# The two half tiles at the end of a fused attention-and-MLP kernel write their results into another pair of SBUF buffers

## The chip, the cores and the metric

The kernel runs on one core of a Trainium2 chip. The metric is device time in microseconds for one execution, from start to end, the median of several runs. The engines of the core that matter here are TensorE (PE, matrix products into PSUM), VectorE (DVE, which reads PSUM and writes SBUF), and SyncE (SP), whose queue issues nearly all DMA transfers, the stores of the output among them.

## The reference, cut to what matters

The input `x` has 2048 tokens of 512 numbers in bf16. It is normalised per token, and two branches read the result: an attention with a running memory (32 heads of 16, four segments of 512 tokens, causal softmax inside a segment, a memory of the earlier segments mixed in by a gate), and an MLP with SiLU (512 to 1792 to 512). The output is the sum of both and `x`.

```python
def _A_ref(x, wq, wk, wv, wo, beta):
    ...
    for s in range(N):                                   # N = 4 segments of L = 512
        p = _softmax(einsum('bhqd,bhkd->bhqk', qs, ks) * scale + mask, axis=-1)
        a_dot = einsum('bhqk,bhkd->bhqd', p, vs)
        num = einsum('bhld,bhde->bhle', phi(qs), M)
        den = einsum('bhld,bhd->bhl', phi(qs), z)[..., None] + 1e-06
        outs.append(g * (num / den) + (1.0 - g) * a_dot)
        M = M + einsum('bhld,bhle->bhde', phi(ks), vs)
        z = z + einsum('bhld->bhd', phi(ks))
    ...
    return o @ wo

def _B_ref(x, w1, w2):
    return _silu(x @ w1) @ w2

x = A_x
xn = _layernorm(x, axis=-1)
return x + _A_ref(xn, A_wq, A_wk, A_wv, A_wo, A_beta) + _B_ref(xn, B_w1, B_w2)
```

## The kernel before, in words

The 2048 tokens are 16 token tiles of 128, four to each of the four segments (`s` = 0 to 3, `j` = 0 to 3 inside a segment). Every matrix product is computed with 128 rows on the partitions. The last step for a token tile adds 18 products in one PSUM bank: 14 of the MLP (`hT`, one for each 128 of the 1792 hidden numbers, with `w2_sb`) and 4 of the attention (`oT` with `wo_sb`). `out_mm` (line 624) issues one such product, whole or in parts; `product` (line 329) splits it into four matmuls of 32 columns of the weights where the neighbouring products do so too, and at the end of the kernel all are split so (line 334).

When the 18 products of a tile are in, one VectorE instruction reads the bank, halves it, adds the residual `x` and writes bf16 into an SBUF buffer (line 617 in `store`), and SyncE issues a DMA from this buffer to the output in HBM (line 622). The last tile of the last segment (`s` = 3, `j` = 3) is done in two halves of 256 output columns instead: the words `oh<i>.<h>` are its products (`half_out`, line 656) and `sh0` and `sh1` its two stores (`half_store`, line 659: VectorE at line 664, the DMA at line 668). Half 0, half 1 and tile 2 lie in banks of their own of one PSUM tile (`psS`, line 637 and 638), and `declare_no_dep` (line 652) says that products in one of these banks need not wait for VectorE's reading of another.

SBUF buffers come from pools. A name (or `tag`) in a pool stands for a fixed number of equal buffers that are handed out in turn: whoever asks for one when all have been used gets the one that was handed out longest ago, and its first writer has to wait until the last reader of the old contents is done. The waits are put in by the framework, as semaphore waits on the instruction. In the pool `work`:

- `o_out` has 3 buffers of 128 x 512 bf16. They are used for the output tiles (line 616), and in the kernel before also for the two halves (line 663). The last reader of the old contents is a store's DMA, so the wait is for its completion.
- `pos` has 2 buffers (the pool's default) of 128 x 512 bf16. They hold the positive part of keys or queries: GpSimd writes it (line 413 in `phi_pos`), and VectorE reads it soon after (line 429 in `phi_sum`).

The order of all work is written out by hand: the string `ORDER` (lines 16 to 90) is a list of words, each word names a piece and its numbers, and the loop at line 900 issues the pieces in this order; each engine then runs its own instructions in that order. No scheduler moves them. The end of the string, cut to the words of the end:

```
... o3.0.15 st3.0 o3.2.17 o3.2.15 oh7.1 st3.2 od3.1.11.3 oh8.0 oh16.1 o3.1.17 o3.1.2 oh3.0 oh17.1 oh12.0 st3.1
oh4.1 oh15.0 oh17.0 oh1.0 oh16.0 sh0 oh3.1 oh10.1 oh15.1 oh0.1 oh5.1 sh1
```

So the last five output buffers are handed out to the tiles 0, 2 and 1 of the last segment (`st3.0`, `st3.2`, `st3.1`), to half 0 (`sh0`) and to half 1 (`sh1`), in this order. With three buffers in turn, half 0 gets the buffer of tile 0, and half 1 that of tile 2.

Of the kernel before, what the change touches and what calls it, by code (L numbers as in the profile page):

```python
# [10 lines left out]
BF16 = mybir.dt.bfloat16  # L11
# [82 lines left out]
def kernel(  # L94
# [15 lines left out]
    P = 128  # L110
    S = 2048
    D = 512
# [5 lines left out]
    L = S // NSEG  # L118
# [12 lines left out]
    work = ctx.enter_context(tc.tile_pool(name="work", bufs=2))  # L131
# [527 lines left out]
    def half_store(h):  # L659

        st, j, cols = sts[LAST], TPS - 1, slice(h * D // 2, (h + 1) * D // 2)
        assert len(st.pop(("done", j, h))) == 4 * (FT + DT)
        o_half = work.tile([P, D], BF16, name="o_half", tag="o_out", bufs=3)[:, 0 : D // 2]
        out = nc.vector.scalar_tensor_tensor(
            out=o_half, in0=st["psO", j, h], scalar=0.5, in1=st["x", j][:, cols], op0=ALU.mult, op1=ALU.add
        )
        fin_out.append(((j, h), out))
        nc.sync.dma_start(out=out_flat[(NT - 1) * P : NT * P, cols], in_=o_half)
# [188 lines left out]
    def keep_busy(n):  # L857
# [21 lines left out]
        "o": out_mm, "oh": half_out,  # L879
        "oc": lambda s, j, i, c: out_mm(s, j, i, None, c, 2), "od": lambda s, j, i, c: out_mm(s, j, i, None, c, 4),  # L880
        "sh": half_store, "xl": load_res, "st": out_store,
        "xs": ln_stats, "xc": ln_sums, "xd": ln_var, "xg": ln_root, "xq": ln_sqrt, "xi": ln_inv, "tb": first_exp,
        "Nv": lambda t: ln_norm(t, nc.vector), "Na": lambda t: ln_norm(t, nc.gpsimd),
# [55 lines left out]
```

## Time and profile before

| | |
|---|---|
| time before, median of 3 runs | 221.58 us (221.27 to 221.88) |
| the profiled execution: its own time | 221.36 us |
| the profiled execution: span from the first to the last instruction | 219.7 us |
| granted TensorE clock, mean over the span | 0.999 |
| PE busy | 211.5 us, 96% of the span |
| DVE busy | 181.2 us, 82% of the span |
| output stores of full tiles (line 622) | 15 of 128 KB |
| output stores of the halves (line 668) | 2 of 64 KB |

The times are of one execution on the chip, seen by the hardware profiler. The span is shorter than the run's time by 1.7 us, which lie before its first and behind its last instruction. A row of the timeline has the start and the length of a group of instructions in microseconds, then the engine, the line in the kernel, the operation, what it writes and what it reads, the shapes, and how many instructions are in the group (x4). An engine's name with a q behind it (SPq, DVEq) is that engine's instruction queue: the issuing of a DMA, a wait on a semaphore. In square brackets stands how long the engine had been idle before, and whose work ended this. The chain of work that ended last is followed back from the last instruction that counts as busy; DMAs that run on behind that instruction are not in it.

### The profile page before, as it was taken

Reading aid. Unit: us, or ns where it says so; the run is one execution under the profiler, and the core shown is the slowest. Engines: PE = TensorE matmul, PEld = TensorE weight load, DVE = VectorE, ACT = ScalarE, POOL = GpSimd, SP = SyncE. Lnnn points to the kernel's source line nnn. Section 1 sums busy time; section 2 is a strip of 40 time slices with the busy share of each in tenths; the row PEclk is TensorE's granted clock in tenths of the full one; section 3 lists DMA queues with packets and bytes.
Section 4 is the critical chain, followed back from the end, with each engine's and each line's share of the span. In section 5 each row is a group of like instructions: output and inputs, shape, how many; then the busy total and the mean of one; then the engine's idle time right before and its main releaser. Section 6 shows DMA issues by size and latency. Waiting matters only on the chain.

```text
span 219.7 us, 9344 instructions
## 1 busy us (share of the span) xinstructions
PE 211.5 (96%) x4019; PEld 116.2 (53%) x4042; DVE 181.2 (82%) x370; ACT 184.3 (84%) x173; POOL 126.8 (58%) x203
## 2 busy tenths in 40 slices
PE   7999999999999999999999999999999999999993
PEld 7666655556544444445544445555454554465662
DVE  7899899998897878766988978777899898678463
ACT  3899989999999999999999999999999998850000
POOL 6039986679687845695845586676768472410000
PEclk9999999999999999999999999999999999999999
DMA  5994549241003033221122141250032222312212
GB/s 185 364 387 116 78 112 345 57 82 44 3 4 75 27 90 86 68 56 31 48 75 63 46 116 28 50 76 7 4 96 88 66 75 51 99 52 86 88 51 97
DMA packets 32745, 19.60 MB, mean 89 GB/s; under 512 B 14656, under 2 KB 32192, under 8 KB 32704
## 3 DMA queue, kind: packets, MB, share of 16 engines
q1 hardware_dynamic: 30080, 16.39, 27.8%
q10 hardware_dynamic: 2624, 2.62, 3.8%
q8 instruction: 31, 0.51, 1.0%
q14 instruction: 10, 0.08, 0.1%
HBM read 9.96 MB, written 2.10 MB: 55 GB/s over the span
## 4 chain that ended last, share of the span: by engine, by line
PE 80%; DVE 10%; POOL 4%; issue 2%; DMA 1%; ACT 1%; DVEq 0%
PE ps L332 20%; PE psO L334 16%; PE ps L334 15%; PE psS L720 9%; PE psO L332 9%; PE psV L787 8%; PE psS L334 3%; DVE stats L282 2%; POOL Pb L740 2%; DVE Vz L402 1%; POOL k L381 1%; DMA out_dram<-o_out 1%; DVE hT L493 1%; DVE pk L429 1%; POOL lows L740 1%
## 5 line engine op out<-in xcount | busy, mean ns | idle before, releaser
L726 ACT ACTIVATE Pb<-psS 128x2048 bf16<-128x2048 f32 x72 | 135.2, 1877 | 6.2 <-PE psS L720 4.1
L740 POOL TENSOR_SCALAR_AFFINE_SELECT Pb<-Pb 128x512 bf16<-128x512 bf16 (+2 forms) x88 | 61.6, 709 | 19.4 <-ACT Pb L726 16.6
L493 DVE SCALAR_TENSOR_TENSOR hT<-th,ps 128x512 bf16<-128x512 bf16 x56 | 37.9, 680 | 10.4 <-ACT th L488 10.0
L740 POOL TENSOR_SCALAR_AFFINE_SELECT lows<-Pb 64x512 bf16<-64x512 bf16 (+1 forms) x40 | 23.2, 580 | 37.4 <-ACT Pb L726 31.0
L334 PE MATMUL psO<-w_sb,hT 128*32 128x512 bf16 (+2 forms) x708 | 43.3, 321 | 0.0
L332 PE MATMUL ps<-xnT,w_sb 128*128 128x512 bf16 (+1 forms) x165 | 34.2, 329 | 0.4 <-DVE Vz L402 0.2
L488 ACT ACTIVATE th<-ps 128x512 bf16<-128x512 f32 x56 | 33.2, 594 | 1.7 <-PE ps L334 1.6
L334 PEld LDWEIGHTS <-hT 128*32 128x32 bf16 x876 | 21.6, 97 | 14.0 <-issue 2.6
L334 PE MATMUL ps<-xnT,w_sb 128*32 128x512 bf16 (+1 forms) x448 | 26.4, 348 | 0.0
L720 PE MATMUL psS<-qT,k 32*128 32x64 bf16 (+3 forms) x512 | 23.0, 233 | 0.5 <-ACT Pb L726 0.3
L332 PEld LDWEIGHTS <-w_sb 128*128 128x128 bf16 x168 | 15.8, 98 | 11.5 <-issue 1.0
L787 PE MATMUL psV<-Pb,Vz 128*32 128x448 bf16 (+7 forms) x512 | 21.6, 286 | 0.2 <-POOL Pb L740 0.2
L720 PEld LDWEIGHTS <-k 32*128 32x128 bf16 x512 | 9.4, 92 | 22.8 <-issue 22.2
L332 PE MATMUL psO<-w_sb,hT 128*128 128x512 bf16 (+2 forms) x82 | 20.9, 326 | 0.6 <-issue 0.5
L787 PEld LDWEIGHTS <-Vz 128*32 128x32 bf16 x768 | 16.2, 97 | 9.3 <-issue 0.8
L617 DVE SCALAR_TENSOR_TENSOR o_out<-psO,x_res 128x512 bf16<-128x512 f32 x14 | 9.7, 690 | 6.6 <-PE psO L334 4.9
L334 PEld LDWEIGHTS <-w_sb 128*32 128x32 bf16 x448 | 11.1, 96 | 7.4 <-issue 1.6
L720 PE MATMUL psS<-qT,kT 16*128 16x448 bf16 (+3 forms) x256 | 14.7, 269 | 0.0
L817 DVE CAST oraw<-psV 128x512 bf16<-128x512 f32 x15 | 10.2, 682 | 3.1 <-PE psV L787 3.0
L402 DVE CAST Vz<-ps 128x512 bf16<-128x512 f32 x15 | 10.2, 681 | 2.8 <-PE ps L334 1.6
L332 PEld LDWEIGHTS <-hT 128*128 128x128 bf16 x89 | 7.8, 98 | 8.7 <-issue 2.2
L332 PE MATMUL ps<-xnT,wq_sb 128*128 128x256 bf16 (+1 forms) x59 | 12.1, 322 | 0.2 <-issue 0.2
(113 smaller groups left out, 333.5 us busy)
## 6 DMA issues: line engine op xcount, KB each, us to landing
spr<-rz SPq DMA_DIRECT2D x56, 64.0 KB
x_res<-in_A_x_dram SPq DMA_DIRECT2D x16, 128.0 KB
out_dram<-o_out SPq DMA_DIRECT2D x15, 128.0 KB
w_sb<-in_B_w_dram SPq DMA_DIRECT2D x1, 1792.0 KB
w_sb<-in_B_w_dram ACTq DMA_DIRECT2D x1, 1792.0 KB
x_hi<-in_A_x_dram SPq DMA_DIRECT2D x2, 512.0 KB
wv_sb<-in_A_wv_dram SPq DMA_DIRECT2D x2, 256.0 KB
wk_sb<-in_A_wk_dram SPq DMA_DIRECT2D x1, 512.0 KB
```

Of the source, the lines that this page charges most:

```text
L282: nc.vector.bn_stats(out=stats[t][:], in_=xs(t, t + 1)[:, 0, :])
L332: return [nc.tensor.matmul(out, lhsT=lhsT, rhs=rhs, start=start, stop=stop, skip_group_check=True)]
L334: nc.tensor.matmul(out[c : c + 32], lhsT=lhsT[:, c : c + 32], rhs=rhs, start=start, stop=stop, tile_position=(0, c), skip_group_check=True,)
L402: copy(out=Vzs[s % 2][:, j, :, 0:3:2, :], in_=sts[s].pop(("v", j))[:, :].rearrange("p (h r d) -> p h r d", r=2, d=DH),)
L488: nc.scalar.activation(out=th[:], in_=sts[s]["h", ft][:, :], func=AF.Tanh, scale=0.5)
L493: nc.vector.scalar_tensor_tensor(out=st["hT"][:, ft, :], in0=st.pop(("th", ft))[:], scalar=1.0, in1=st.pop(("h", ft))[:, :], op0=ALU.add, ...
L617: out = nc.vector.scalar_tensor_tensor(out=o_out[:], in0=st.pop(("psO", j)), scalar=0.5, in1=st["x", j][:], op0=ALU.mult, op1=ALU.add)
L720: nc.tensor.matmul(psS[:, g, c : c + q2 - q1], lhsT=keys[rows], rhs=st["qT"][rows, dt, q1:q2], start=True, stop=True, tile_position=(32 * ...
L726: exp = nc.scalar.activation(out=blocks(Pb, b).rearrange("p y g c -> p g y c"), in_=psS[:, :, :].rearrange("p g (y c) -> p g y c", c=BLOCK ...
L740: over[id(Pb)].append(nc.gpsimd.affine_select(out=out, in_=in_, compare_op=ALU.is_ge, fill=0.0, base=base, pattern=[[0, out.shape[1]], [1, ...
L787: nc.tensor.matmul(psV[32 * g : 32 * g + 32, q0 : q0 + nq].rearrange("p (y c) -> p y c", y=weights.shape[2]), lhsT=Vzs[s % 2][:, kt, 4 * d ...
L817: copy(out=oraw[:], in_=sts[s].pop(("psV", 0))[:, :])
```

## The change

Only line 663 differs. The buffer of a half is no longer taken from the three of `o_out`, but from the two of `pos`. The size of the buffer, the 256 of its 512 columns that are used, the instructions that write and store it, and their order stay.

```diff
         st, j, cols = sts[LAST], TPS - 1, slice(h * D // 2, (h + 1) * D // 2)
         assert len(st.pop(("done", j, h))) == 4 * (FT + DT)
-        o_half = work.tile([P, D], BF16, name="o_half", tag="o_out", bufs=3)[:, 0 : D // 2]
+        o_half = work.tile([P, L], BF16, name="o_half", tag="pos")[:, 0 : D // 2]
         out = nc.vector.scalar_tensor_tensor(
             out=o_half, in0=st["psO", j, h], scalar=0.5, in1=st["x", j][:, cols], op0=ALU.mult, op1=ALU.add
         )
```

`L` and `D` are both 512. The order of instructions on every engine is the same in both kernels; the two VectorE instructions of line 664 wait for PE, for an earlier VectorE instruction and for one DMA each in the kernel before, and for PE alone in the changed one.

## The prediction

> **What bounds the kernel now.** I read the head of the page first, then the chain of waits at its end, the timeline of the last microseconds by engine, and the transfers in slices. The page's head gives engines and span:
>
> ```profile
> span 219.7 us, 9344 instructions
> PE 211.5 (96%) x4019; PEld 116.2 (53%) x4042; DVE 181.2 (82%) x370; ACT 184.3 (84%) x173; POOL 126.8 (58%) x203
> ```
>
> TensorE is busy for 96% of the span, so it bounds the kernel nearly everywhere. The change doesn't touch its stream, but it touches the stretch in which TensorE no longer bounds. The chain of work that ended last, from 213 us on, as start, length and what:
>
> ```profile
> 213.47 0.02 issue
> 213.50 0.70 DVE o_out L617
> 214.20 0.02 issue
> 214.21 2.01 DMA out_dram<-o_out
> 216.22 0.03 issue
> 216.25 0.05 DVEq L664
> 216.30 0.04 issue
> 216.35 0.27 DVE o_half L664
> 216.61 0.08 issue
> 216.69 0.41 DVE o_half L664
> ```
>
> The chain leaves TensorE at 213.47. It runs through the eviction of tile 0, then through the whole store of tile 0 (2.01 us from its issue to its landing), and only then into the two evictions of the halves. A store stands on the path to a VectorE instruction because that instruction writes into the buffer that the store reads. The waits of the last 7 us say the same (the total in us, how often, the longest), and the row of line 664 gives the durations of its two evictions (least, median, most, in ns):
>
> ```profile
> DVE o_half L664 <- DMA out_dram<-o_out: 0.9, 1, 0.9
> L664 DVE SCALAR_TENSOR_TENSOR o_half<-psS,x_res x2: 414/418/423, 216.3 to 216.7; 128x256 bf16<-128x256 f32 x2
> ```
>
> VectorE sits idle for 0.9 us ahead of half 0. Now TensorE's last rows, and VectorE's and SyncE's:
>
> ```profile
> 215.28 0.28 PE L334 MATMUL psS<-wo_sb,oT 128*32 128x256 bf16 x4
> 215.39 0.39 PE L334 MATMUL psS<-w_sb,hT 128*32 128x256 bf16 x8
> 215.61 0.28 PE L334 MATMUL psS<-wo_sb,oT 128*32 128x256 bf16 x4
> 215.72 0.39 PE L334 MATMUL psS<-w_sb,hT 128*32 128x256 bf16 x8
> ...
> 214.74 0.69 DVE L617 SCALAR_TENSOR_TENSOR o_out<-psO,x_res 128x512 bf16<-128x512 f32 x1
> ...
> 215.46 0.33 SPq L622 DMA_DIRECT2D out_dram<-o_out  x1
> 216.80 0.33 SPq L668 DMA_DIRECT2D out_dram<-o_half  x1
> 217.22 0.38 SPq L668 DMA_DIRECT2D out_dram<-o_half  x1
> ```
>
> Read beside the order of the words, the row at 215.28 is the last product of half 0, number 16. The 20 matmuls from 215.39 on are the five products of half 1 behind it. So half 0 is complete in PSUM at 215.28 + 0.28 = 215.56, and half 1 at 215.72 + 0.39 = 216.11. VectorE has nothing to do from 214.74 + 0.69 = 215.43 on, and yet the halves start at 216.35 and 216.69. It is the buffer that both wait for, not the data.
>
> **The change part by part.** It moves no instruction on any queue: VectorE, SyncE, TensorE, ScalarE and GpSimd issue the same work in the same order. It takes the DMA wait (and the wait on an earlier VectorE write) off the two instructions of line 664. What is left is the wait for TensorE.
>
> *The new buffers.* The two `pos` buffers were last written by GpSimd and last read by VectorE. The rows of that tile, with first and last start at the end of the list of numbers:
>
> ```profile
> L413 POOL TENSOR_SCALAR pos<-qT x12: 607/614/616, 38.8 to 166.1; 128x512 bf16<-128x512 bf16 x12
> L429 DVE SCALAR_TENSOR_TENSOR phiQT<-ex,pos x12: 677/684/983, 46.7 to 170.8; 128x512 bf16<-128x512 bf16 x12
> ```
>
> The last reader starts at 170.8 us and takes at most 0.98 us, so both buffers have been free for over 40 us, and there are two of them for two halves: neither half waits for a store again. Nobody asks for a `pos` buffer behind the halves, so no one else is held up. Taking these buffers costs nothing.
>
> *Half 0.* It starts when TensorE's product 16 is in. What lies between a product's end and the eviction that waits for it: in the chain above TensorE ends at 213.47 and VectorE starts at 213.50; by the timeline, the row of that product and one earlier case:
>
> ```profile
> 213.05 0.39 PE L334 MATMUL psO<-wo_sb,oT 128*32 128x512 bf16 x4
> ...
> 213.50 0.69 DVE L617 SCALAR_TENSOR_TENSOR o_out<-psO,x_res 128x512 bf16<-128x512 f32 x1 [1.74 <-PE psO L334]
> ...
> 204.28 0.60 PE L334 MATMUL psO<-w_sb,hT 128*32 128x512 bf16 x8
> 204.94 0.69 DVE L617 SCALAR_TENSOR_TENSOR o_out<-psO,x_res 128x512 bf16<-128x512 f32 x1 [2.02 <-PE psO L334]
> ```
>
> 213.50 - 213.44 = 0.06 and 204.94 - 204.88 = 0.06. So half 0 starts at 215.62, ends 0.42 later at 216.04, and its store is issued 0.03 later (before: 216.35 + 0.42 = 216.77, issue at 216.80), at 216.07. SyncE's queue is free by then: the store of tile 1 ahead of it ends issuing at 215.46 + 0.33 = 215.79. Issuing takes 0.33 and the queue needs another 0.09 to the next (217.22 - 216.80 - 0.33), so it is ready for half 1's store at 216.49.
>
> *Half 1.* It starts at 216.11 + 0.06 = 216.17 (VectorE is free at 216.04), ends 0.41 later at 216.58, and its store is issued at 216.61. Before, that issue was at 217.22. So the last store leaves 0.61 us earlier. The bounds: if the eviction starts at the modelled end of the product itself, 0.67; if it needs 0.12 instead of 0.06 and 0.42 instead of 0.41, 0.54. I take 0.61, because both rows of the hand-over give 0.06.
>
> *The reading beside the writing.* Half 0 is now read from PSUM while TensorE still writes half 1 into another bank; before, TensorE had long stopped. Tile 1 is evicted at 214.74 in the same way, beside 256-wide products at their usual pace (0.11 us for each, from the row at 215.28 to that at 215.39 as from 215.61 to 215.72). I cost this at nothing; if it slowed the 20 last matmuls by a tenth, it would be 0.05.
>
> *The stores.* From the issue of the last store to the end of the span it is 219.7 - 217.22 = 2.48 us: start-up, data, receipt, and the closing barrier. Does this stay 2.48 when the halves come sooner behind the full tiles? The last three columns of the slices are granted clock, share of the DMA engines and GB/s:
>
> ```profile
> 215.50:215.70 0.20, 0.20 (x16) 0.20 (x8) 0.00 (x0) 0.00 (x0) 0.00 (x0) 1.00 0.22 67
> ...
> 216.70:216.90 0.20, 0.00 (x0) 0.00 (x0) 0.20 (x2) 0.00 (x0) 0.00 (x0) 1.00 0.09 26
> ...
> 217.50:217.70 0.20, 0.00 (x0) 0.00 (x0) 0.00 (x0) 0.00 (x0) 0.00 (x0) 1.00 0.21 61
> ...
> 218.30:218.50 0.20, 0.00 (x0) 0.00 (x0) 0.00 (x0) 0.00 (x0) 0.00 (x0) 1.00 0.32 85
> ```
>
> In the first slice, between two full ones, tile 0's store ends its data and tile 2's begins. The data of tile 1's store are through at about 216.75. Half 0's begin at about 217.65, 0.85 us behind their issue, and half 1's are through by about 218.4; the 0.42 us between the two issues were enough to keep the two apart. With the change half 0's data begin at 216.07 + 0.85 = 216.92, still behind tile 1's, and half 1's at 217.46, 0.54 behind. All gaps stay positive, so 2.48 stays, and the store costs nothing more. Were that cover gone and half 0 queued behind tile 1 entirely, half 0 alone would be later, by up to its own 0.3 us of data, and half 1 by less than that.
>
> One rule speaks against this. The Trainium skill, "DMA: Bandwidth & Descriptors", section "Latency and other measured facts", says that an access to HBM takes 0.2 us on average but 2 us at high load, and that the receipt of a write carries this time. If four or five stores in close sequence are "high load", the sum by this rule would be a loss (it stands below as a rival's form); by the rows above it is the gain of 0.61. No run here shows a receipt of 2 us.
>
> *The sum.* 219.7 - 0.61 = 219.09 for the span. The profiled execution took 221.36, 0.22 under the median; 221.36 - 0.61 = 220.75, and the median of 221.58 becomes 220.97. That is 0.28% less, just inside the 0.3% (0.66 us) which is about what a measurement of this kernel can tell from no change; the three runs lie 0.61 us apart.
>
> **The rivals.**
>
> *The receipts of the stores take the wait's place.* Tile 0's store landed at 216.22. By the first slice above its data were through at about 215.55: 0.67 us of receipt, with another store right behind it. The last store's receipt was shorter; a row of the waits at the kernel's end (least, median, most in ns, first and last start):
>
> ```profile
> L934 SPq DRAIN  x3: 7/7/13, 218.9 to 219.2; - x3
> ```
>
> SyncE's first drain, behind its waits for the last stores, is at 218.9: 0.5 us behind the data's end at 218.4. If the nearer neighbours bring the last receipt to 0.67, 0.17 of the gain go: 221.58 - 0.44 = 221.14. For it speaks that the pause of 0.75 us on the DMA engines ahead of the halves vanishes; against it that half 1, the last, has nothing behind it.
>
> *The halves' stores are held until tile 1's store has landed, and the end is later than before.* The place is the way of the two stores to HBM. Tile 1's store, issued at 215.46, lands about 2.01 later, at 217.47. In the kernel before, the halves come so late (216.80) that most of this is over; in the changed one half 0 comes 1.4 us ahead of it. If stores with the next store close behind them hold up the followers until they are acknowledged, half 0 leaves as if issued at 217.47 and half 1 0.42 later at 217.89, and the span ends at 217.89 + 2.48 = 220.37: 221.58 + 0.67 = 222.25. It decides from the point at which half 1's store is held beyond 217.22. Against it speaks that tile 2's data began at about 215.7, half a microsecond ahead of tile 0's landing at 216.22; for it, that no store in this trace stands as close behind two others as half 0 then would with a small one right behind.
>
> The page's form of this rival is the HBM rule of the Trainium skill, "DMA: Bandwidth & Descriptors": with its 2 us as the last receipt in place of 0.5, an estimate from that page, the time would be 221.58 - 0.61 + 1.5 = 222.47.
>
> *More than the sum.* TensorE's ends are modelled. If the hand-over for the narrow products is 0.05 shorter and the closing barrier, which other engines enter earlier, gives another 0.1, the gain is 0.76: 220.82.
>
> *The change doesn't do what it says.* If the `pos` buffers had a late reader, the wait would stay: 221.58. The rows end at 171.8 us, so hardly.
>
> **How the numbers follow.** The forecast (0.61, with 0.54 to 0.67) gets 0.80. It ends 0.05 us short of the bound of 0.66 while single runs scatter over 0.61 us, so I halve it: 0.40 faster, 0.40 the same. More than the sum: 0.07, faster. Receipts: 0.04, the same. Held stores: 0.08, slower. No effect: 0.01, the same. That makes 0.47 faster, 0.45 the same, 0.08 slower. The time is the forecast's, 220.97. The range takes the scatter of the runs shown (0.3 to either side) around 220.97, the larger gain below (220.82 less 0.27) and the receipts above (221.14 plus 0.3): 220.55 to 221.44. The held stores and the tail of the scatter are what is left out.
>
> **What the profile of the changed kernel would show.** Right: no wait of line 664 on a DMA; half 0 at about 215.62 and half 1 at about 216.17, both released by TensorE; the issues of line 668 at 216.07 and 216.61; the chain leaving TensorE at about 216.1 and not at 213.47; the last store's issue to the span's end still about 2.5 us. The receipts: the same starts, but an end above 219.2. The held stores: a gap on the DMA engines between the halves' issues and their data well over 0.85 us, and an end beyond 219.7. Wrong altogether: line 664 waiting for VectorE or GpSimd, or TensorE's last products spread beyond 216.11.

## The result and the profile after

| | before | changed |
|---|---|---|
| median of 22 runs each | 221.75 us | 221.05 us |
| lowest and highest | 221.27 to 222.33 | 220.69 to 222.41 |
| ratio of the times, 95% interval | | 0.9977 (0.9966 to 0.9987) |

The changed kernel is faster by 0.51 us as the ratio has it, by 0.29 to 0.75 us as its interval has it (0.0013 and 0.0034 of 221.75). The medians differ by 0.70 us. The kernel before was measured anew beside it; its median of three runs, from which the prediction counted, was 221.58.

The profiled execution of the changed kernel is one of its longer ones (221.99 us, the second longest of 22), and its span of 220.3 us is longer than the 219.7 before. So the two traces can't be compared by the clock on the wall; they are compared from the start of tile 0's eviction on, 213.50 before and 214.77 after. Where the 1.27 us ahead of that point went is told in the last section. The chain of waits of the changed kernel, its last three pieces (start, length, what):

```profile
215.96 1.45 PE psS L334 x52
217.41 0.02 issue
217.43 0.42 DVE o_half L664
```

Before, the chain left TensorE at the end of tile 0 and went through a store. Now it stays with TensorE to the last product and has one eviction behind that. The timeline of the same stretch, TensorE, VectorE and SyncE:

```profile
216.55 0.28 PE L334 MATMUL psS<-wo_sb,oT 128*32 128x256 bf16 x4
216.66 0.39 PE L334 MATMUL psS<-w_sb,hT 128*32 128x256 bf16 x8
216.88 0.28 PE L334 MATMUL psS<-wo_sb,oT 128*32 128x256 bf16 x4
216.99 0.39 PE L334 MATMUL psS<-w_sb,hT 128*32 128x256 bf16 x8
...
214.77 0.69 DVE L617 SCALAR_TENSOR_TENSOR o_out<-psO,x_res 128x512 bf16<-128x512 f32 x1 [1.74 <-PE psO L334]
216.89 0.97 DVE L664 SCALAR_TENSOR_TENSOR o_half<-psS,x_res 128x256 bf16<-128x256 f32 x2 [0.18 <-PE psS L334]
...
217.34 0.88 SPq L668 DMA_DIRECT2D out_dram<-o_half  x2
217.88 0.33 SPq L668 DMA_DIRECT2D out_dram<-o_half  x1
```

The last row is the second of the two issues in the row above it, from a narrower window.

Half 0's last product ends at 216.55 + 0.28 = 216.83 and its eviction starts at 216.89; half 1's ends at 216.99 + 0.39 = 217.38 and its eviction starts at 217.43. VectorE's idle time ahead of the halves fell from 0.9 to 0.18 us, and TensorE ends it. TensorE's rows keep their 0.11 us for each product while half 0 is read beside them.

Counted from the start of tile 0's eviction: the last store was issued at 217.22 - 213.50 = 3.72 us before, and is issued at 217.88 - 214.77 = 3.11 us now. That is 0.61 us earlier. From that issue to the end of the span it is 220.3 - 217.88 = 2.42 us (before 2.48; the spans are rounded to 0.1).

The DMA slices of the changed kernel (the last two columns are the share of the DMA engines and GB/s):

```profile
217.90:218.10 0.20, 0.00 (x0) 0.00 (x0) 0.00 (x0) 0.00 (x0) 0.00 (x0) 1.00 0.37 118
218.10:218.30 0.20, 0.00 (x0) 0.00 (x0) 0.00 (x0) 0.00 (x0) 0.00 (x0) 1.00 0.49 143
218.30:218.50 0.20, 0.00 (x0) 0.00 (x0) 0.00 (x0) 0.00 (x0) 0.00 (x0) 1.00 0.66 185
218.50:218.70 0.20, 0.00 (x0) 0.00 (x0) 0.00 (x0) 0.00 (x0) 0.00 (x0) 1.00 0.00 0
218.70:218.90 0.20, 0.00 (x0) 0.00 (x0) 0.00 (x0) 0.00 (x0) 0.00 (x0) 1.00 0.78 228
218.90:219.10 0.20, 0.00 (x0) 0.00 (x0) 0.00 (x0) 0.00 (x0) 0.00 (x0) 1.00 0.37 100
```

Tile 1's data end in the first of them, half 0's lie in the second and third, and half 1's come after a pause in the last two. The pause ahead of half 0 has gone; no slice shows the stores in each other's way.

### The profile page after: what moved, and what is told of

It is laid out like the page before. It is cut to its first block, busy times and chain, and to the rows that moved or that the text cites. A ratio compares the mean times of both kernels' runs of the same rounds, so it can differ in the third digit from the quotient of the medians.

```text
span 220.3 us, 9365 instructions
## 1 busy us (share of the span) xinstructions
PE 214.5 (97%) x4042; PEld 117.3 (53%) x4042; DVE 181.8 (83%) x370; ACT 184.2 (84%) x173; POOL 127.3 (58%) x203
## 4 chain that ended last, share of the span: by engine, by line
PE 87%; DMA 7%; ACT 3%; issue 0%; SPq 0%; DVE 0%
PE ps L332 21%; PE psO L334 17%; PE ps L334 16%; PE psS L720 11%; PE psO L332 10%; PE psV L787 8%; DMA w_sb<-in_B_w_dram 6%; PE psS L334 4%; ACT Pb L726 3%; DMA x_lo<-in_A_x_dram 1%; PE psM L448 1%; PE ps L505 0%; ACT th L488 0%; SPq L158 0%; DVE o_half L664 0%
## 5 line engine op out<-in xcount | busy, mean ns | idle before, releaser
L332 PE MATMUL psO<-w_sb,hT 128*128 128x512 bf16 (+2 forms) x89 | 22.3, 331 | 0.0
L332 PE MATMUL ps<-xnT,wq_sb 128*128 128x256 bf16 (+1 forms) x62 | 12.8, 325 | 0.0
```

Source lines behind the costliest of these rows:

```text
L332: return [nc.tensor.matmul(out, lhsT=lhsT, rhs=rhs, start=start, stop=stop, skip_group_check=True)]
```

## The experiments

In all of them but the last, TensorE, ScalarE and GpSimd do the same work in the same order as in the changed kernel. Times are set beside the kernel before, measured on the same chip in the same series; positions are counted from the start of tile 0's eviction.

**Half 0 alone gets a free buffer.**

```diff
-        o_half = work.tile([P, L], BF16, name="o_half", tag="pos")[:, 0 : D // 2]
+        o_half = work.tile([P, D], BF16, name="o_half", tag=("pos", "o_out")[h], bufs=(2, 3)[h])[:, 0 : D // 2]
```

> Half 0 takes a buffer of pos, half 1 one of o_out; with half 0 out of the turn, half 1 gets the buffer of tile 0. My theory (each half waits for the landing of the store that reads its buffer, and the last issue sets the end): half 0 starts 0.06 us after its last product; half 1 starts when tile 0's store has landed, 2.01 us after the issue of that store, plus 0.13 for the hand-over, which is 2.85 us after the start of tile 0's eviction (before: half 1 at 3.19 after it, changed: 2.66). Last issue 0.43 us earlier than before: 221.75 - 0.43 = 221.3. Rival (half 0 alone holds the end, since it stands ahead of half 1 in the queue): the whole gain of the change, 221.1. Rival (both must be free): no gain, 221.75.

221.28 us against 221.72 (ratio 0.9980, 0.9969 to 0.9991). The end of its chain of waits:

```profile
213.83 0.70 DVE o_out L617
214.53 0.02 issue
214.55 1.87 DMA out_dram<-o_out
216.42 0.03 issue
216.45 0.05 DVEq L664
216.50 0.04 issue
216.54 0.42 DVE o_half L664
```

With half 0 out of the turn, half 1 has tile 0's buffer instead of tile 2's. It starts when tile 0's store has landed (1.87 us after its issue) plus 0.12. That is 216.54 - 213.83 = 2.71, only 0.05 behind the 217.43 - 214.77 = 2.66 of the changed kernel. I had expected 2.85 with a landing of 2.01. The position is that of my theory with a shorter landing; the time, 0.44 less in the medians, fits the expected 0.43, but can't tell it from the 0.6 of the rival. The last issue comes 216.99 - 213.83 = 3.16 behind the start of tile 0's eviction, 0.56 earlier than before and not 0.43. Nor does the position decide, for TensorE was done at nearly the same time:

```profile
216.05 0.39 PE L334 MATMUL psS<-w_sb,hT 128*32 128x256 bf16 x8
216.54 0.42 DVE L664 SCALAR_TENSOR_TENSOR o_half<-psS,x_res 128x256 bf16<-128x256 f32 x1 [0.17 <-PE psS L334]
```

Half 1's last product ends at 216.44, so without any store half 1 would have started at about 216.50, only 0.04 earlier; the timeline names TensorE as what ended the wait, the chain the store. And since half 1 got another buffer here, the run doesn't show what freeing half 0 alone does while half 1 keeps tile 2's.

**Half 1 alone gets a free buffer.**

```diff
-        o_half = work.tile([P, L], BF16, name="o_half", tag="pos")[:, 0 : D // 2]
+        o_half = work.tile([P, D], BF16, name="o_half", tag=("o_out", "pos")[h], bufs=(3, 2)[h])[:, 0 : D // 2]
```

> Half 0 keeps the buffer of tile 0, half 1 takes one of pos. My theory: half 0 still waits for the landing of tile 0's store, and half 1 stands behind it in VectorE's queue, so it starts 0.3 to 0.34 us behind half 0 and the last issue moves by 0.00 to 0.04: 221.75, no gain. Rival (the last store hangs on half 1's own wait for the store of tile 2): the gain of the change, 221.1.

221.75 us against 221.72 (ratio 1.0008, 0.9991 to 1.0025): no gain. Its rows, VectorE's and SyncE's:

```profile
213.66 0.69 DVE L617 SCALAR_TENSOR_TENSOR o_out<-psO,x_res 128x512 bf16<-128x512 f32 x1 [1.74 <-PE psO L334]
216.47 0.76 DVE L664 SCALAR_TENSOR_TENSOR o_half<-psS,x_res 128x256 bf16<-128x256 f32 x2 [0.87 <-DMA out_dram<-o_out]
...
217.34 0.39 SPq L668 DMA_DIRECT2D out_dram<-o_half  x1
```

Half 1 is free to go 0.5 us earlier, but it stands behind half 0 on VectorE, which still waits for the store. The last issue is at 217.34 - 213.66 = 3.68, nearly the 3.72 before. So half 0's wait for the store of tile 0, at the head of VectorE's queue, is enough to hold the end. Whether half 1's own wait, for the store of tile 2, would be enough too is read from the next run.

**The wait made longer: the halves write into the buffers of tiles 2 and 1.**

```diff
-        o_out = work.tile([P, D], BF16, name="o_out", bufs=3)
+        o_out = st["o", j] = work.tile([P, D], BF16, name="o_out", bufs=3)
 ...
-        o_half = work.tile([P, D], BF16, name="o_half", tag="o_out", bufs=3)[:, 0 : D // 2]
+        o_half = st["o", (2, 1)[h]][:, 0 : D // 2]
```

Unlike the other edits, this one is shown against the kernel before.

> Before, with the wait made longer: half 0 writes into the buffer of tile 2 and half 1 into that of tile 1, whose stores leave 0.6 and 1.25 us behind that of tile 0. My theory: half 1 starts 0.13 us behind the landing of tile 1's store (issue of that store + 1.75 to 2.01), and the last issue comes 0.56 to 0.82 us later than before: 222.3 to 222.6. Rival (the receipts or the closing barrier set the end, and the halves' start has some slack): less than 0.2 us later, under 221.95.

222.36 us against 221.72 (ratio 1.0032, 1.0021 to 1.0042), so 0.64 us more in the medians, inside the expected 0.56 to 0.82. The end of its chain:

```profile
216.11 0.02 issue
216.13 1.70 DMA out_dram<-o_out
217.83 0.03 issue
217.86 0.05 DVEq L664
217.91 0.04 issue
217.95 0.43 DVE o_out L664
```

Now half 1 waits for tile 1's store, which lands 1.70 us after its issue. The last issue is at 218.40 - 214.16 = 4.24, 0.52 later than before; that is just short of the expected 0.56, since the landing was put at 1.75 or more. There is no slack behind the halves: what the landing costs arrives at the end.

The same trace shows what a wait for tile 2's store alone does, with nothing held ahead of it. Here it is half 0 that has this wait:

```profile
214.16 0.69 DVE L617 SCALAR_TENSOR_TENSOR o_out<-psO,x_res 128x512 bf16<-128x512 f32 x1 [1.74 <-PE psO L334]
...
217.37 0.42 DVE L664 SCALAR_TENSOR_TENSOR o_out<-psS,x_res 128x256 bf16<-128x256 f32 x1 [1.26 <-DMA out_dram<-o_out]
```

It starts 217.37 - 214.16 = 3.21 behind the start of tile 0's eviction. In the kernel before, half 1 started 216.69 - 213.50 = 3.19 behind it. So half 1's own wait, left alone, would have held the end at about the same place: by these positions the kernel before had two waits that ended together, and both had to go. A run with half 0 freed and half 1 still on tile 2's buffer wasn't made.

**Another free pair.**

```diff
-        o_half = work.tile([P, L], BF16, name="o_half", tag="pos")[:, 0 : D // 2]
+        o_half = work.tile([P, L], BF16, name="o_half", tag="ex")[:, 0 : D // 2]
```

> Both halves take buffers of the pair of the exponentials, ex, free since 171 us as pos is. My theory (any free pair does it): the same as the changed kernel, 0.5 to 0.7 us under before, 221.05 to 221.25, both halves released by TensorE 0.05 to 0.06 us after their last product. Rival (something about pos itself, its address or its late readers): another time, by over 0.2 us.

221.06 us against 221.72 (ratio 0.9966, 0.9953 to 0.9979; 8 runs): as the changed kernel, 221.05. The halves start at 216.55 and 217.10, tile 0's eviction at 214.43, which is 2.12 and 2.67 (changed: 2.12 and 2.66). Nothing hangs on `pos` itself.

**One free buffer for both halves.**

```diff
-        o_half = work.tile([P, L], BF16, name="o_half", tag="pos")[:, 0 : D // 2]
+        o_half = work.tile([P, D], BF16, name="o_half", tag="zsum", bufs=1)[:, 0 : D // 2]
```

> Both halves share one buffer, that of zsum, free for long: half 0 waits for TensorE alone, half 1 for the landing of half 0's store. My theory (a wait costs what the landing of the store in the buffer costs, and a 64 KB store alone behind others lands in 1.5 to 1.7 us): half 1 starts 0.13 us behind that landing, the last issue comes 0.9 to 1.15 us later than before: 222.65 to 222.85. Rival (a small store close behind full ones takes as long as theirs, 1.9 to 2.0, or is held up by them): 1.3 us or more, 223.0 or above. Rival (half 1's wait has slack, as the old pair of waits had): under 222.2.

222.66 us against 221.66 (ratio 1.0052, 1.0032 to 1.0072; 6 runs), 1.00 more in the medians. The end of its chain:

```profile
215.99 0.44 DVE o_half L664
216.42 0.02 issue
216.44 1.53 DMA out_dram<-o_half
217.97 0.03 issue
218.00 0.05 DVEq L664
218.05 0.04 issue
218.09 0.42 DVE o_half L664
```

Half 0's store of 64 KB, issued 0.6 us behind tile 1's, lands in 1.53 us. This store, close behind three larger ones, is not held up. Half 1 starts 0.12 behind its landing, and the last issue is at 218.55 - 213.87 = 4.68, 0.96 later than before.

**The neighbours' stores left out.**

```diff
-        nc.sync.dma_start(out=out_flat[t * P : (t + 1) * P, :], in_=o_out[:])
+        s == LAST and j in (1, 2) or nc.sync.dma_start(out=out_flat[t * P : (t + 1) * P, :], in_=o_out[:])
```

> The changed kernel without the stores of tiles 1 and 2 of the last segment (these 256 rows of the output aren't written). My theory (the halves' stores run freely, the neighbours cost nothing): from the issue of the last store to the end of the span 2.35 to 2.45 us, as in the changed kernel, and the time that of the changed kernel within 0.2: 220.9 to 221.25. Rival (the receipts of close stores, or load on HBM, lengthen the last store): shorter by 0.17 us or more in that stretch, and the time 220.85 or less.

221.19 us against 221.66 (ratio 0.9982, 0.9968 to 0.9995). SyncE's last issue in this kernel:

```profile
216.94 0.33 SPq L668 DMA_DIRECT2D out_dram<-o_half  x1
```

The span ends at 219.4, 2.46 us behind it, against 2.42 with the neighbours: with spans rounded to 0.1 that is no difference, and not 0.17 less. The neighbours' stores cost the last one nothing that these two traces resolve.

**The load of w1 in two parts** belongs to the scatter of the runs, not to the change.

```diff
-    load_w(nc.sync, w1_sb, B_w1, 0, DT)
+    for f0, f1 in ((8, FT), (0, 8)): nc.sync.dma_start(out=w1_sb[:, :, f0 * P : f1 * P], in_=B_w1.rearrange("(ko ki) n -> ki ko n", ki=P)[:, :, f0 * P : f1 * P])
```

> The changed kernel with the load of w1 in two parts, the columns of the hidden numbers 1024 to 1791 (0.79 MB) first, the rest behind them; nothing is left out. In the profiles of the changed kernel and of ex_pair TensorE idles 0.9 to 1.0 us at 17 us until w1 has landed, in six others it doesn't, and what is lost there is still lost at the end. My theory (that wait makes the scatter of the runs, in all kernels alike, and has nothing to do with the halves): no wait for w1 at the first product that reads it (words h0.11), in the profile the third exponential 2.4 us behind the second, and the runs near the lower end of the changed kernel's: median 220.75 to 221.05, most runs under 221.4. Rival (the second part lands late instead, at h0.5): the same scatter, a wait for w1 at about 18 us. Rival (the early microseconds get worse, the loads behind w1 come late): median over 221.3.

221.21 us (220.77 to 222.05, 12 runs) against 221.88 (ratio 0.9977, 0.9960 to 0.9994). The wait for w1 isn't in its profile, but the runs still scatter over 1.28 us (the 22 of the changed kernel over 1.72, the 8 of the `ex` pair over 0.99), and the median lies above the 220.75 to 221.05 that my theory expected. So the theory that this wait makes the scatter missed; what is left of it stands in the last section.

## Why the prediction was right

*The sum.* Forecast was 0.61 us, 220.97 against 221.58. The trace shows 0.61 from issue to issue, and the runs 0.51 (0.29 to 0.75), 221.05 in the median. The kernel is faster, but by 0.23%, within the bound of 0.3%; that is the case of the forecast which I had given half of its chance. The kernel before came out 0.17 longer than the 221.58 from which the prediction counted; from its 221.75, the forecast's 0.61 would give 221.14.

*Half 0 and half 1.* The hand-over from TensorE was forecast at 0.06 and measures 0.06 and 0.05; the positions 215.62 and 216.17 were 2.12 and 2.67 behind the start of tile 0's eviction, and 2.12 and 2.66 came out. The last issue was forecast 3.11 behind it (216.61 - 213.50), and is 3.11. That these starts, and not something behind them, set the end is shown by the two kernels with longer waits: +0.64 and +1.00 us in the medians, where the last issue came 0.52 and 0.96 later.

*The buffers.* That it is not `pos` itself is shown by the pair `ex`, which does the same. That both halves wait for their buffers and not for the data was read rightly; the prediction doesn't say that either wait alone would have held the end, which the run with half 1 freed shows for half 0's wait and the 3.21 of the run with the longer wait makes likely for half 1's.

*The reading beside the writing.* Costed at nothing; TensorE's last rows keep 0.11 us for each product.

*The stores.* The 2.48 us from the last issue to the end stayed (2.42). The rival of longer receipts would have needed 0.17 more with the neighbours than without; it is 0.04 less, which is within the rounding of the spans. The rival of stores held until tile 1's landing is excluded by the run with one buffer: there tile 1's store, issued 0.6 ahead of half 0's 216.44, would land at about 217.5 with the 1.70 that the run with the longer wait shows (an estimate), and half 0's store landed at 217.97, 1.53 us after its own issue and too early for a store that set out at 217.5. The page's form of that rival goes by the Trainium skill, "DMA: Bandwidth & Descriptors", section "Latency and other measured facts", which has 2 us for an access to HBM at high load. In this case the stores whose landing a chain of waits shows took 1.53 to 2.01 us as a whole, from issue to landing, so none of these receipts came near 2 us.

*What was off.* Tile 1's store was put at 2.01 us to its landing, after tile 0's; it lands after 1.70, and tile 0's itself after 2.01, 1.97 and 1.87 in three traces. The change's own sum didn't use that figure, so nothing followed; the rival that was built on it was priced too high.

*More than the sum* did not come: neither the hand-over nor the closing barrier gave more than rounding.

## What to carry to other kernels

A buffer pool's turn is a wait on whoever read the old contents, and at the end of this kernel that reader is a store of 1.5 to 2 us that no later work hides. It doesn't take more memory to cure it: look for a pair whose last reader is long done. And where two waits stand in one queue, look at both. Here freeing the later one alone brought nothing (221.75 against 221.72). Freeing the earlier one alone, with half 1 left on tile 2's buffer, was not run; by the start of 3.21 with that buffer against 3.19 before, it should bring nothing either. The run that freed half 0 gained because half 1 got an older buffer by it, whose store landed just as TensorE was done.

## What was not expected: where the runs differ

Up to tile 0's eviction the first eight kernels here (before, changed, and all but the last of the experiments) issue the same work, and yet their profiled executions start tile 0's eviction between 213.50 and 214.77. In the trace of the changed kernel 0.94 us of this were lost at one place; the first product that reads w1, in the changed kernel:

```profile
17.89 0.61 PE L332 MATMUL ps<-xnT,w_sb 128*128 128x256 bf16 x4 [0.94 <-DMA w_sb<-in_B_w_dram]
```

and in the kernel before, where it starts 1.52 us earlier:

```profile
16.37 0.60 PE L332 MATMUL ps<-xnT,w_sb 128*128 128x256 bf16 x4
```

In two of the first eight profiles (the changed kernel and the `ex` pair) TensorE had to wait 0.9 to 1.0 us for w1, in the other six it didn't; the load lands at about the time at which it is first needed. I took this for the cause of the scatter. The split load shows that it can't be the whole of it: its profiled execution is one of its longer ones (221.62 us, the fourth longest of 12) and yet has no such wait,

```profile
17.14 0.60 PE L332 MATMUL ps<-xnT,w_sb 128*128 128x256 bf16 x4
```

but earlier ones for the weights of values and keys, which the trace of the changed kernel doesn't have,

```profile
PEld L332 <- DMA wk_sb<-in_A_wk_dram: 0.5, 1, 0.5
PE ps L332 <- DMA wv_sb<-in_A_wv_dram: 0.4, 1, 0.4
```

and the runs still spread over 1.3 us. So in these profiles the waits for the first loads differ from execution to execution by about as much as this change is worth. Only one execution of each kernel has a profile, so which of these waits makes most of the scatter, if they make it, stays open.
